# One low-rank product of three matmuls, moved by two steps in TensorE's program

## The chip, the core and the metric

The kernel runs on one core of a Trainium2 chip. The metric is device time in microseconds (us), taken over repeated runs; the profiled execution gives the trace. Ratios are computed as the mean time of one kernel's fast runs over that of the other's fast runs of the same rounds, so they are not quite the ratio of the medians quoted beside them.

## The reference

For each of 8 batches (3136 rows, 256 columns): squared-ReLU attention gated by `u`, then a mixer with a rank-32 product over the rows and a two-layer ReLU network over the columns.

```python
scores = (1 / S) * z @ z.T                  # z: 3136 x 64
x = u * (np.maximum(scores, 0) ** 2 @ v)    # attention, gated
h = x.T @ U @ V                             # rank 32 over the rows
y = x + h.T
out = y + np.maximum(y @ w_ch1, 0) @ w_ch2  # 256 -> 1024 -> 256
```

## The kernel before

The attention of batch b and the mixer of batch b - 1 are interleaved by hand: the order in which the program emits instructions is the order on each engine. The 3136 rows are 25 tiles, so a batch has 25 outputs of 25 steps each; a step is two matmuls, one on each half of TensorE's rows. Outputs come in pairs, and a pair accumulates in one of two sets of two banks of PSUM, the memory that takes TensorE's results (`ps` in the traces). The set that is not in use is "spare": the low-rank products of the mixer borrow it. (`...` stands for lines left out, and the pieces stand apart in the kernel.)

```python
def spare():
    return sets[(opened[0] + (0 if acc else 1)) % 2]

def open_pair(b, o):                        # at step 0 of a pair: takes the spare set
    acc[pair_of(o)[0]] = sets[opened[0] % 2]
    opened[0] += 1

def low_rank(b, c, ps=None, turned=True):   # the rank-32 product of one chunk of tiles
    ts = chunks[c]                          # four tiles; three in chunk 3; two in chunk 6
    ps = spare() if ps is None else ps
    where = [(0, 0), (1, 0)] if len(ts) == 2 else [(0, 0), (0, 1), (1, 0), (1, 1)]
    order = sorted(zip(where, ts), key=lambda e: (e[0][1], e[0][0]))
    for (h, k), t in order:                 # h: bank and row half, k: half of the bank
        mm(out=ps[h][:, k * D : (k + 1) * D],
           lhsT=V_bf[halves[h], col(t) : col(t) + P], rhs=t1[b][halves[h], :],
           start=True, stop=True)
    ...
    for h in range(2):                      # VectorE reads bank 0, then bank 1
        ...
        nc.vector.tensor_tensor(out=q, in0=split(ps[h][:, : len(ks) * D]), in1=q, op=ALU.add)
    if turned:
        turn_x(b, c)                        # DMA transpose for the next layer

def _spread(main, filler):                  # score pieces, spread over an output's steps
    n, m = len(main), len(filler)
    k = 0
    for i, step in enumerate(main):
        step()
        while k < m and (2 * k + 1) * n <= (i + 1) * 2 * m:
            filler[k]()
            k += 1
    ...

# in the loop over batches b and outputs i:
ahead = dict(zip((2, 3, 6, 7, 10, 11, 14), range(NC)))    # output -> chunk
main = attend_steps(b, o)
if b and i in ahead:
    main.insert(17 if (i + (i > FIRST)) % 2 == 0 else 10, lambda c=ahead[i]: low_rank(b - 1, c))
_spread(main, fill)
```

So the third chunk's product stands late in output 6 and the fourth's at entry 10 of output 7, and both use the same spare set. A score piece is two matmuls (L298), a ReLU on ScalarE (L311) and a square on VectorE (L313).

## Time and profile before

| | before |
|---|---|
| median of the first three runs | 1002.39 us (1002.05 to 1003.09) |
| profiled span | 998.3 us |
| TensorE busy | 983.4 us, 99% |
| VectorE, ScalarE busy | 551.1 us, 612.2 us |

Read it as: TensorE sets the time, and only its own waits can be won. In the traces the line of an instruction tells what it is: L371 an output step, L298 a score piece, L531 a low-rank product, L545 its additions on VectorE, L405 the steps of output 12 (the tail tile), L563 and L610 the two layers of the mixer's network. `A` holds the squared scores, a `strip` is a part of `A` transposed by a DMA, `ut` is the mixer's input transposed by a DMA, and `o_sb` is the buffer from which the output is stored.

One measure is the time **from the start of the first chunk's product (output 2) to the start of the fifth's (output 10)** of the same batch. It holds the place of the change, and repeats to 0.01 us where nothing stray hits it. In the kernel before, the seven batches have 49.50, 49.50, 49.50, 49.51, 50.21, 49.50 and 49.50 us.

### The profile page before, as it was taken

Reading aid. Unit: us, or ns where it says so; the run is one execution under the profiler, and the core shown is the slowest. Engines: PE = TensorE matmul, PEld = TensorE weight load, DVE = VectorE, ACT = ScalarE, POOL = GpSimd, SP = SyncE. Lnnn points to the kernel's source line nnn. Section 1 sums busy time; section 2 is a strip of 40 time slices with the busy share of each in tenths; the row PEclk is TensorE's granted clock in tenths of the full one; section 3 lists DMA queues with packets and bytes.
Section 4 is the critical chain, followed back from the end, with each engine's and each line's share of the span. In section 5 each row is a group of like instructions: output and inputs, shape, how many; then the busy total and the mean of one; then the engine's idle time right before and its main releaser. Section 6 shows DMA issues by size and latency. Waiting matters only on the chain.

```text
span 998.3 us, 31020 instructions
## 1 busy us (share of the span) xinstructions
PE 983.4 (99%) x13688; PEld 776.5 (78%) x13688; DVE 551.1 (55%) x1003; ACT 612.2 (61%) x835; POOL 171.7 (17%) x317
## 2 busy tenths in 40 slices
PE   8899999999999999999999999999999999999998
PEld 6678777787778877788787887878877788787866
DVE  6878754467444665456644566445664457542352
ACT  8877764667645776466754667556674666643154
POOL 5111112111121211221112211112111120011000
PEclk9999999999999999999999999999999999999999
DMA  9999989899798999999999997989979998678533
GB/s 195 185 195 204 174 156 186 185 176 173 153 198 171 169 157 186 179 178 169 160 180 176 181 168 149 188 174 177 175 151 194 166 188 159 120 150 161 129 95 101
DMA packets 414790, 167.94 MB, mean 168 GB/s; under 512 B 389488, under 2 KB 399408, under 8 KB 414656
## 3 DMA queue, kind: packets, MB, share of 16 engines
q1 hardware_dynamic: 385424, 99.68, 62.3%
q0 software_dynamic: 29232, 66.28, 28.3%
q8 instruction: 107, 1.75, 0.7%
q14 instruction: 27, 0.22, 0.1%
HBM read 61.88 MB, written 25.69 MB: 88 GB/s over the span
## 4 chain that ended last, share of the span: by engine, by line
PE 91%; DVE 4%; ACT 3%; DMA 1%; issue 1%; POOL 0%; DVEq 0%; POOLq 0%
PE ps L371 47%; PE ps L563 17%; PE ps L610 17%; PE ps L298 6%; ACT A L311 2%; DVE A L313 2%; PE ps L405 1%; PE ps L531 1%; DVE x_bf L545 1%; DMA out_dram<-o_sb 1%; DMA strip<-A 1%; DVE both L386 1%; PE ps L479 1%; DVE x_bf L395 1%; PE ps L207 0%
## 5 line engine op out<-in xcount | busy, mean ns | idle before, releaser
L311 ACT ACTIVATE A<-ps 128x832 bf16<-128x832 f32 (+9 forms) x477 | 358.9, 769 | 155.4 <-PE ps L298 148.1
L371 PE MATMUL ps<-v,A 64*128 64x256 bf16 x4988 | 341.6, 269 | 1.8 <-DVE A L313 1.1
L313 DVE TENSOR_TENSOR A<-A 128x832 bf16<-128x832 bf16 (+9 forms) x477 | 244.7, 527 | 133.1 <-ACT A L311 130.0
L371 PE MATMUL ps<-v,strip 64*128 64x256 bf16 x4420 | 307.3, 269 | 3.4 <-DMA strip<-A 2.5
L371 PEld LDWEIGHTS <-A 64*128 64x128 bf16 x4988 | 246.3, 94 | 45.4 <-issue 10.0
L581 ACT ACTIVATE relu_bf<-ps 128x1024 bf16<-128x1024 f32 (+2 forms) x206 | 186.2, 911 | 140.0 <-PE ps L563 139.8
L371 PEld LDWEIGHTS <-strip 64*128 64x128 bf16 x4420 | 222.6, 94 | 37.2 <-DMA strip<-A 3.9
L624 DVE TENSOR_TENSOR o_sb<-ps,x_bf 128x512 f32<-128x512 f32 (+2 forms) x105 | 69.9, 665 | 243.7 <-PE ps L610 221.7
L610 PE MATMUL ps<-w_bf,relu_bf 128*128 128x256 bf16 (+1 forms) x1600 | 201.2, 273 | 0.0
L563 PE MATMUL ps<-ut,w_bf 128*128 128x512 bf16 (+2 forms) x896 | 198.6, 353 | 0.0
L610 PEld LDWEIGHTS <-relu_bf 128*128 128x128 bf16 (+1 forms) x1600 | 153.0, 98 | 45.6 <-issue 3.6
L563 PEld LDWEIGHTS <-w_bf 128*128 128x128 bf16 x896 | 84.9, 98 | 62.0 <-issue 6.9
L355 POOL DMA_DIRECT2D u_sb<-in_u_dram x96 | 53.7, 559 | 456.1 <-DVE x_bf L395 441.9
L298 PE MATMUL ps<-zT 64*128 64x416 bf16 (+8 forms) x812 | 131.6, 312 | 0.0
L385 ACT COPY both<-ps 128x512 f32<-128x512 f32 (+1 forms) x104 | 58.9, 566 | 72.9 <-PE ps L371 66.6
L637 POOL DMA_DIRECT2D out_dram<-o_sb x84 | 46.0, 548 | 276.2 <-DVE o_sb L624 272.9
L386 DVE TENSOR_TENSOR both<-ps,both 128x512 f32<-128x512 f32 (+1 forms) x104 | 69.3, 667 | 28.2 <-ACT both L385 27.5
L395 DVE TENSOR_TENSOR x_bf<-both,u_sb 128x512 bf16<-128x512 f32 (+1 forms) x104 | 69.8, 672 | 3.7
L545 DVE TENSOR_TENSOR x_bf<-ps,x_bf 128x512 bf16<-128x512 f32 (+1 forms) x112 | 65.5, 626 | 7.2 <-PE ps L531 7.1
L298 PEld LDWEIGHTS <-zT 64*128 64x128 bf16 x812 | 43.1, 94 | 4.0
L244 POOL DMA_DIRECT2D v<-in_v_dram x61 | 34.1, 561 | 0.8 <-DMA w_bf<-in_moe_w_ch_dram 0.7
L298 PE MATMUL ps<-relu_bf 64*128 64x416 bf16 (+9 forms) x121 | 22.2, 333 | 3.9 <-ACT A L311 3.3
(54 smaller groups left out, 208.0 us busy)
## 6 DMA issues: line engine op xcount, KB each, us to landing
u_sb<-in_u_dram POOLq DMA_DIRECT2D x96, 256.0 KB, 4.1
out_dram<-o_sb POOLq DMA_DIRECT2D x84, 256.0 KB, 3.3
v<-in_v_dram POOLq DMA_DIRECT2D x57, 192.0 KB, 4.8
strip<-A SPq DMA_TRANSPOSE x196, 5.5
out_dram<-o_sb SPq DMA_DIRECT2D x11, 256.0 KB, 2.0
z_c<-in_z_dram POOLq DMA_DIRECT2D x7, 384.0 KB, 5.9
u_sb<-in_u_dram POOLq DMA_DIRECT2D x16, 64.0 KB, 2.5
ut<-x_bf SPq DMA_TRANSPOSE x56, 3.7
```

Source lines behind the costliest of these rows:

```text
L298: mm(out=ps[:, k, :n], lhsT=zT[halves[k], j, :], rhs=zT_flat[halves[k], c : c + n], start=True, stop=True,)
L311: nc.scalar.activation(out=dst, in_=src, func=AF.Relu, scale=sc)
L313: nc.vector.tensor_tensor(out=dst, in0=dst, in1=dst, op=ALU.mult)
L371: mm(out=acc[t0][h][:, (o - t0) * D : (o - t0 + 1) * D], lhsT=w[halves[h]], rhs=v_both[b % 2][halves[h], j, :], start=start, stop=stop, **kw,)
L385: nc.scalar.copy(out=both[:, :w], in_=banks[1][:, :w])
L386: nc.vector.tensor_tensor(out=both[:, :w], in0=banks[0][:, :w], in1=both[:, :w], op=ALU.add)
L395: nc.vector.tensor_tensor(out=x_at(b, t0, n), in0=split(both[:, :w]), in1=u_sb[:, :n, :].rearrange("p t (a c) -> p t a c", c=P), op=ALU.mult,)
L545: nc.vector.tensor_tensor(out=q, in0=split(ps[h][:, : len(ks) * D]), in1=q, op=ALU.add)
L563: mm(out=ps[i][:, :w] if apart else ps[:, i, :w], lhsT=w1_bf[:, db, (hp + i) * P : (hp + i + 1) * P], rhs=uT[c][:, db, len(chunks[c]) * P ...
L581: nc.scalar.activation(out=relus[c][:, hp : hp + 2, :w], in_=ps[:, :, :w], func=AF.Relu)
L610: mm(out=ps[r, k * D : (k + 1) * D], lhsT=relus[c][:, ht, q : q + (TAIL if two else P)], rhs=w2_bf[:, ht, :], start=(ht < 1 + two), stop=( ...
L624: nc.vector.tensor_tensor(out=o_sb[:p].rearrange("p t (a c) -> p t a c", c=P), in0=split(ps[:p, k0 * D : (k + 1) * D]), in1=x_at(b, t, nk) ...
```

## The change

The intent: the fourth chunk's product stands at TensorE waiting for its banks; put it two steps later and let those steps run in front of it.

```diff
             main = attend_steps(b, o)
             if b and i in ahead:
-                main.insert(17 if (i + (i > FIRST)) % 2 == 0 else 10, lambda c=ahead[i]: low_rank(b - 1, c))
+                at = 17 if (i + (i > FIRST)) % 2 == 0 else 12 if i == 7 else 10
+                main.insert(at, lambda c=ahead[i]: low_rank(b - 1, c))
             _spread(main, fill)
```

## The prediction

> **What bounds the kernel now.** I read the page first, then the list of waits of the whole run, then the waits of TensorE alone in stretches, then the timeline around the instruction that the diff moves, for all seven batches that have it. The page:
>
> ```profile
> span 998.3 us, 31020 instructions
> PE 983.4 (99%) x13688; PEld 776.5 (78%) x13688; DVE 551.1 (55%) x1003; ACT 612.2 (61%) x835; POOL 171.7 (17%) x317
> PEclk9999999999999999999999999999999999999999
> PE 91%; DVE 4%; ACT 3%; DMA 1%; issue 1%; POOL 0%; DVEq 0%; POOLq 0%
> ```
>
> TensorE is busy for 99% of the span at the full granted clock, and 91% of the chain that ended last is TensorE. Every other engine has 39% or more free. So time is gained only where TensorE does less work or stands still for less time. That it stands still so rarely makes its few waits readable one by one. The complete list for TensorE's matmuls is:
>
> ```profile
> PE ps L298 <- ACT A L311: 3.3, 5, 1.0
> PE ps L371 <- DMA strip<-A: 2.5, 1, 2.5
> PE ps L371 <- DVE A L313: 2.0, 4, 0.9
> PE ps L207 <- DVE zT L204: 1.3, 1, 1.3
> PE ps L531 <- DVE x_bf L545: 1.1, 7, 0.2
> PE ps L371 <- DVE o_sb L624: 0.5, 1, 0.5
> PE ps L298 <- ACT relu_bf L231: 0.4, 1, 0.4
> ```
>
> (Columns: total us, times, longest.) Asked in stretches of the span, the start-up before 80 us holds all of these but two: one wait of 0.5 us near 645 us, and the row of L531. L531 is the low-rank product, and seven waits fit batches 1 to 7, each of which holds the product that the diff moves. The timeline of TensorE and of VectorE in batch 2 shows it (start, duration, engine, line):
>
> ```profile
> 258.43 0.71 PE L371 MATMUL ps<-v,A 64*128 64x256 bf16 x10
> 258.98 0.27 PE L531 MATMUL ps<-t_sb,V_bf 64*128 64x256 bf16 x1
> 259.40 0.29 PE L531 MATMUL ps<-t_sb,V_bf 64*128 64x256 bf16 x2 [0.16 <-DVE x_bf L545]
> 259.51 0.40 PE L371 MATMUL ps<-v,A 64*128 64x256 bf16 x4
> 259.73 0.33 PE L298 MATMUL ps<-zT 64*128 64x352 bf16 x2
> ```
>
> ```profile
> 258.67 0.68 DVE L545 TENSOR_TENSOR x_bf<-ps,x_bf 128x512 bf16<-128x512 f32 x1
> ```
>
> The fourth chunk's product has three matmuls. The first, into bank 0 of the spare pair, starts at 258.98. The second, into bank 1, starts only at 259.40, 0.05 us after VectorE ends (258.67 + 0.68 = 259.35) the second addition of the THIRD chunk's product, which used the same two banks half an output earlier. It is a wait for a buffer. The same pair of starts, 0.42 to 0.43 us apart, stands in all seven batches (137.77 and 138.19 in the first, 865.97 and 866.39 in the last), so one figure holds for all.
>
> How much does a site lose? Not the 0.16 us in brackets: that counts only from the modelled end of the first matmul (258.98 + 0.27). A full product of four matmuls in the same batch starts at 256.62, and the next output matmul at 256.83: 0.21 us for four, in two side-by-side pairs. Here three matmuls need the same two turns, so the next output matmul should start near 258.98 + 0.21 = 259.20 and starts at 259.51. **Loss: 0.31 us a site, 7 x 0.31 = 2.2 us in all.** No change to this wait can give more.
>
> **What the Trainium skill says.** "PSUM — Partial Sum Buffer", section "PSUM bank collisions raise a hardware error", asks for semaphores by bank: a matmul may not write a bank while VectorE reads it. The trace agrees: the first matmul (bank 0, freed 0.6 us earlier) goes, the second waits, and only until the addition that reads its bank is over. "TensorE: Matmul & The Clock Gate", section "The mechanism", says that matmuls are strict FIFO. So independent output matmuls that stand behind the blocked one in the program can't overtake it; the trace agrees, as the L371 matmuls at 259.51 need nothing from it and still come after. This is why order in the program matters here at all. "Perfetto Trace Analysis", section "Tensor Engine Instruction (MATMUL, LD_WEIGHTS)", says that a matmul's end is estimated and not observed; hence I count from start to start, and the bracket's 0.16 against 0.31 is this case's measure of the difference.
>
> **The change part by part.** It removes and adds no instruction. `at` becomes 12 instead of 10 for output 7 alone, in batches 1 to 7 (ahead holds chunk 3 there).
>
> (1) Order on TensorE. Output 7 has 25 steps of two matmuls each, one per row half, and with the product 26 entries. Three score pieces are spread over it (1408 columns in two, 256 in one): by the rule in _spread they follow entries 4, 12 and 21. Before: steps 0 to 9, product, steps 10 and 11, second score piece, step 12. After: steps 0 to 11, product, second score piece, step 12. So exactly two steps, four matmuls, pass in front of the product.
>
> (2) Order elsewhere. The additions of the product still come after the square of score piece 1 and before that of piece 2 on VectorE; ScalarE, the DMA queues and the transposes keep their order wholly. VectorE's addition that frees the bank hangs on nothing moved, so it still ends near 259.35 on the old clock.
>
> (3) What two steps fill. The trace has x16 output matmuls as 0.87 us from issue to issue (for example in the chain of waits), so a step is 0.87 / 8 = 0.109 us and two are 0.22 us. They would run at 258.98 and 259.09. The first product matmul goes at 259.20, the second still waits until 259.40, the third follows at 259.42, and the score piece starts at about 259.51 where it started at 259.73. **Gain 0.22 us of the 0.31; 0.09 us stays as a wait, because 12 is not quite late enough.**
>
> (4) Does the gain survive what comes next? VectorE doesn't get earlier at once: it squares until about 259.9 and then adds for the product (259.87 to 260.89), set by its own queue. Its next squares were ready to start at 260.89 in any case. At the close of outputs 6 and 7 it has caught up:
>
> ```profile
> 262.09 0.69 DVE L386 TENSOR_TENSOR both<-ps,both 128x512 f32<-128x512 f32 x1 [0.24 <-ACT both L385]
> ```
>
> It idles 0.24 us there for ScalarE, which waits for TensorE; with TensorE 0.22 us earlier this idle shrinks to about nothing and nothing is late. The spare banks are opened for outputs 8 and 9 after 261.9, about 1 us after the product's last addition. Between two such sites TensorE has no listed wait but the single 0.5 us, so nothing is there to take the gain back.
>
> (5) Sum: 7 x 0.22 = 1.5 us. 1002.39 - 1.53 = **1000.9 us**, a gain of 0.15%.
>
> **The rivals.** *A: the wait moves on and nothing is gained.* VectorE is the laggard at this site: the chain of waits runs through two squares and both additions for 2.1 us before it comes back to TensorE, so TensorE catches up on VectorE's schedule, and a gain here could reappear as a wait at the next meeting (close of the pair, bank reuse for output 8). For: that chain. Against: the 0.24 us of VectorE idle at the close, the 1 us of room before the banks are reopened, and that TensorE shows no other wait in a batch. It would leave 1002.4 us. *B: the whole wait goes.* If the time lost beyond the two steps is partly hidden (third matmul overlapped with what follows on the other row half), the gain would be up to 0.31 us a site: 1002.39 - 2.2 = 1000.2 us. For: the remaining 0.09 us is less than one step. Against: the bank is not free before 259.35, and the first product matmul would come at 259.20. *C: the later product delays the third-chunk-to-fourth transposes and so the mixer's first product of chunk 3.* For: the transpose into ut for chunk 3 is issued at 264.78 and takes about 4.1 us to land, near 268.9. Against: its additions are set by VectorE's queue and don't get later; the transpose is then held in its queue by two others (a strip at 260.71, z at 262.93), so even 0.2 us would vanish; and the matmuls that read it start at 271.40, 2.5 us after. It would take a slip of over 2 us; then each 0.1 us more would cost 0.7 us in all. I give it almost nothing. *D: a different order of the same work changes a modelled pattern of row halves.* The product's third matmul uses one row half; what follows is now a score pair instead of an output step, both of which use both halves, so at most a fraction of a step, 0.1 us a site or 0.7 us in all, either way.
>
> **Range and chances.** The whole wait is 2.2 us, 0.2% of the time; no mechanism that I can name reaches 2% (20 us) in either direction. The three runs before spread over 1.0 us (1002.05 to 1003.09), which is two thirds of the predicted gain. The low end is B with a little spread, 1000.0; the high end is A with a little less than no gain, 1002.2. Faster by over 2%: 0.01. Within 2%: 0.98. Slower: 0.01. The question that is really open is whether 1.5 us shows above the spread.
>
> **What the profile after would show.** Step 1: in each of the seven sites the output steps before the product number two more (four matmuls), and a score pair follows the product directly. Step 3: the distance from the first to the second product matmul shrinks from 0.42 to about 0.20 us, less than a matmul's modelled length of 0.27, so the row "PE ps L531 <- DVE x_bf L545" should vanish from the waits although a wait of 0.2 us is still there. Step 4: no new TensorE wait in a batch, and the distance from one batch's site to the next, 121.2 us in the trace before (380.42 to 501.63), shrinks to about 121.0. The seven together: the span falls by about 1.5 us from 998.3. It would be wrong if the distance of batches stays at 121.2 although the gap in the site has shrunk (A), if the score piece after the product waits for something (a new row of L298), or if the up product of chunk 3 shows a wait for ut (C).

## The result, and the profile after

Six runs each: the changed kernel 1001.36 us (998.93 to 1003.71), the kernel before 1002.74 us (1001.74 to 1004.45); ratio 0.9985, 95% interval 0.9966 to 1.0003: the same at 2%. The predicted ratio was 1000.9 / 1002.39 = 0.9985 too, but single runs lie several us apart, so the total alone would prove nothing. The trace does.

The timeline of TensorE at the place of the change, changed kernel, batch 2 (start, duration, engine and line, with the count behind x):

```profile
262.80 0.49 PE L371 MATMUL ps<-v,A 64*128 64x256 bf16 x6
263.12 0.49 PE L531 MATMUL ps<-t_sb,V_bf 64*128 64x256 bf16 x3
263.44 0.33 PE L298 MATMUL ps<-zT 64*128 64x352 bf16 x2
263.59 0.29 PE L371 MATMUL ps<-v,A 64*128 64x256 bf16 x2
```

The product is one group now, with no bracket, and the score pair follows it directly. What was 0.53 us from the first product matmul to the next other matmul (258.98 to 259.51) is 0.32 us here (263.12 to 263.44). Three matmuls need 0.21, so 0.11 us a batch is still lost, without any mark in the trace.

The complete list of TensorE's matmul waits in the changed kernel (us in total, times, longest):

```profile
PE ps L298 <- ACT A L311: 6.1, 6, 2.8
PE ps L371 <- DMA strip<-A: 3.4, 2, 2.4
PE ps L207 <- DVE zT L204: 1.3, 1, 1.3
PE ps L371 <- DVE A L313: 1.1, 3, 0.5
PE ps L223 <- DVE z_bf L188: 0.6, 1, 0.6
PE ps L298 <- ACT relu_bf L231: 0.4, 1, 0.4
PE ps L371 <- DMA v<-in_v_dram: 0.3, 1, 0.3
```

The row of L531 is gone. Everything that is listed lies in the start-up, before 100 us.

First to fifth product: 49.28 us in six of the seven batches (49.57 in the first, where an up product, L563, starts 0.3 us later after the second chunk's product than in the other batches; the trace puts that down to the transpose `ut`, but it is in no list). The clean figures differ by 0.22 us, as predicted; seven times that is 1.5 us.

Yet the span of this very trace is longer: 1000.2 against 998.3 us. Cut it at two products to see where:

| trace | start to first product | from there to the fifth product of batch 7 | rest | span |
|---|---|---|---|---|
| before | 111.29 | 777.70 | 109.31 | 998.3 |
| changed | 115.15 | 775.78 | 109.32 | 1000.2 |

The middle, where the change is, is 1.92 us shorter: 1.5 us of it is the change, and the rest are stray waits that only one of the traces has. The start-up was 3.86 us longer, though the change touches nothing before output 7 of batch 1. Most of it is TensorE's own waiting there: without L531 and o_sb, the listed waits of the kernel before (in the prediction) sum to 9.5 us, those of the changed kernel to 13.2. The chain that ended last, in shares of the span, points at the same stretch. Before:

```profile
PE ps L371 47%; PE ps L563 17%; PE ps L610 17%; PE ps L298 6%; ACT A L311 2%; DVE A L313 2%; PE ps L405 1%; PE ps L531 1%; DVE x_bf L545 1%; DMA out_dram<-o_sb 1%; DMA strip<-A 1%; DVE both L386 1%; PE ps L479 1%; DVE x_bf L395 1%; PE ps L207 0%
```

After:

```profile
PE ps L371 48%; PE ps L610 17%; PE ps L563 17%; PE ps L298 6%; DMA strip<-A 3%; ACT A L311 2%; PE ps L531 1%; PE ps L405 1%; DMA z_c<-in_z_dram 1%; PE ps L479 1%; DVE A L313 1%; DMA ut<-x_bf 0%; DVE both L386 0%; PE ps L462 0%; POOL v L244 0%
```

In the changed kernel's execution the chain runs through DMA for longer (strips 3%, z 1%) than in the other (strips 1%); why, is not shown. The additions L545, 1% of the chain before, are no longer among its lines, which fits the change.

### The profile page after: what moved, and what is told of

Same layout as the page of the kernel before. It is cut to its first block, busy times and chain, and to the rows that moved or that the text cites. A ratio compares the mean times of both kernels' runs of the same rounds, so it can differ in the third digit from the quotient of the medians.

```text
span 1000.2 us, 31020 instructions
## 1 busy us (share of the span) xinstructions
PE 982.9 (98%) x13688; PEld 778.4 (78%) x13688; DVE 551.0 (55%) x1003; ACT 612.5 (61%) x835; POOL 171.6 (17%) x317
## 4 chain that ended last, share of the span: by engine, by line
PE 92%; DMA 4%; ACT 2%; DVE 1%; POOL 0%; issue 0%; DVEq 0%; ACTq 0%; POOLq 0%
PE ps L371 48%; PE ps L610 17%; PE ps L563 17%; PE ps L298 6%; DMA strip<-A 3%; ACT A L311 2%; PE ps L531 1%; PE ps L405 1%; DMA z_c<-in_z_dram 1%; PE ps L479 1%; DVE A L313 1%; DMA ut<-x_bf 0%; DVE both L386 0%; PE ps L462 0%; POOL v L244 0%
## 5 line engine op out<-in xcount | busy, mean ns | idle before, releaser
L371 PE MATMUL ps<-v,A 64*128 64x256 bf16 x4988 | 340.9, 269 | 1.5 <-DVE A L313 1.1
L371 PE MATMUL ps<-v,strip 64*128 64x256 bf16 x4420 | 307.6, 269 | 3.4 <-DMA strip<-A 3.4
L371 PEld LDWEIGHTS <-A 64*128 64x128 bf16 x4988 | 247.7, 94 | 44.0 <-issue 10.2
L371 PEld LDWEIGHTS <-strip 64*128 64x128 bf16 x4420 | 223.8, 94 | 36.4 <-DMA strip<-A 4.5
L624 DVE TENSOR_TENSOR o_sb<-ps,x_bf 128x512 f32<-128x512 f32 (+2 forms) x105 | 69.9, 666 | 241.9 <-PE ps L610 216.9
L563 PE MATMUL ps<-ut,w_bf 128*128 128x512 bf16 (+2 forms) x896 | 198.7, 353 | 0.1
L563 PEld LDWEIGHTS <-w_bf 128*128 128x128 bf16 x896 | 84.8, 98 | 62.4 <-issue 6.7
L545 DVE TENSOR_TENSOR x_bf<-ps,x_bf 128x512 bf16<-128x512 f32 (+1 forms) x112 | 65.5, 626 | 6.9 <-PE ps L531 6.8
```

Source lines behind the costliest of these rows:

```text
L371: mm(out=acc[t0][h][:, (o - t0) * D : (o - t0 + 1) * D], lhsT=w[halves[h]], rhs=v_both[b % 2][halves[h], j, :], start=start, stop=stop, **kw,)
L563: mm(out=ps[i][:, :w] if apart else ps[:, i, :w], lhsT=w1_bf[:, db, (hp + i) * P : (hp + i + 1) * P], rhs=uT[c][:, db, len(chunks[c]) * P ...
L624: nc.vector.tensor_tensor(out=o_sb[:p].rearrange("p t (a c) -> p t a c", c=P), in0=split(ps[:p, k0 * D : (k + 1) * D]), in1=x_at(b, t, nk) ...
```

## The experiments

All outputs are right. In each table row, "first to fifth" is the value of the batches without a stray wait, and "batches" says how many of the seven these are.

| kernel | first to fifth, us | batches | time ratio (95% interval) |
|---|---|---|---|
| before | 49.50 | 6 | 1 |
| changed | 49.28 | 6 | 0.9985 (0.9966 to 1.0003) |
| changed, again | 49.28 | 6 | 0.9994 (0.9974 to 1.0015) |
| changed, a third time | 49.28 | 6 | 0.9969 (0.9932 to 1.0007) |
| `at5` | 50.05 | 7 | 1.0059 (1.0029 to 1.0089) |
| `at13` | 50.19 | 7 | 1.0029 (1.0012 to 1.0046) |
| `thirteen` | 49.17 | 6 | 0.9960 (0.9945 to 0.9976) |
| `thirteen`, again | 49.18 | 5 | 0.9954 (0.9915 to 0.9993) |
| `third_later` | 49.28 | 4 | one look: 1002.79 us |
| `third_later`, again | 49.28 | 4 | one look: 1008.43 us |
| `score_banks` | 49.57 | 6 | one look: 999.96 us |
| `both_sites` | 49.18 | 7 | 0.9990 (0.9974 to 1.0005) |

By the threshold of 2% every one of these ratios is "the same"; what follows rests on the batches.

### at5: the suspected wait made longer

```diff
-                at = 17 if (i + (i > FIRST)) % 2 == 0 else 12 if i == 7 else 10
+                at = 17 if (i + (i > FIRST)) % 2 == 0 else 5 if i == 7 else 10
```

> The fourth chunk's product at entry 5 of output 7, five steps earlier than in the kernel before, instead of two later; the order on VectorE and ScalarE is unchanged. My theory (TensorE stands at the second matmul until VectorE's last addition of the third chunk's product, a time that doesn't depend on where the product stands): every step that no longer stands in front of it adds 0.109 us to the wait, so 0.55 us a batch more than before. From the start of the first chunk's product to that of the fifth's: 49.50 us before, 49.28 in the changed kernel, 50.05 here. Seven waits on L545 of about 0.7 us each after the modelled end (1.1 us in total before, about 5 here). Time: 3.8 us over before (about 1.0038). Rival (VectorE sets the pace here and TensorE only meets it later, so the place of the wait doesn't matter): 49.50 and the time of before.

50.04 or 50.05 us in all seven batches, 0.55 more than before, which is what five steps of 0.109 us give. The timeline of TensorE, batch 2:

```profile
260.40 0.27 PE L531 MATMUL ps<-t_sb,V_bf 64*128 64x256 bf16 x1 [0.21 <-DVE x_bf L545]
261.00 0.28 PE L531 MATMUL ps<-t_sb,V_bf 64*128 64x256 bf16 x2 [0.33 <-DVE x_bf L545]
261.10 0.40 PE L371 MATMUL ps<-v,A 64*128 64x256 bf16 x4
```

Now the first matmul waits as well, for the addition that reads bank 0, and the second for the one that reads bank 1. The list has 14 waits of 3.8 us in all, where I had expected seven of about 5. The decisive number is the second matmul's start counted from the third chunk's product (258.21 here, 256.62 before): 2.79 us here, 2.78 before. In the changed kernel it is 2.79 as well (260.54 to 263.33). The release is at a fixed time; only what stands in front of it changes. The time (1.0059) has the expected 1.0038 inside its interval.

### third_later: what fixes the release

```diff
-                at = 17 if (i + (i > FIRST)) % 2 == 0 else 12 if i == 7 else 10
+                at = (19 if i == 6 else 17) if (i + (i > FIRST)) % 2 == 0 else 12 if i == 7 else 10
```

> The changed kernel with the THIRD chunk's product also two steps later (entry 19 of output 6 in place of 17), so that the two products are again as far apart on TensorE as in the kernel before. My theory (VectorE's queue of squares sets when the additions of the third product end, and TensorE's distance is nothing): VectorE gets to those additions only about 1 us after the matmuls, so the matmuls have room; first to fifth product stays 49.28 us, the second matmul of the fourth product still starts 0.2 us after the first, no wait listed on L545. Rival (it is the distance of the two products that counts): 49.50, and the 0.42 us and the seven listed waits return.

The distance from the third to the fourth product on TensorE is now 2.36 us (258.23 to 260.59), as it was before the change (256.62 to 258.98). Still the gain stands: 49.28 us, and the product is one group without a listed wait.

```profile
258.23 0.38 PE L531 MATMUL ps<-t_sb,V_bf 64*128 64x256 bf16 x4
258.53 1.02 DVE L313 TENSOR_TENSOR A<-A 128x768 bf16<-128x768 bf16 x2
259.47 1.28 DVE L545 TENSOR_TENSOR x_bf<-ps,x_bf 128x512 bf16<-128x512 f32 x2
260.59 0.49 PE L531 MATMUL ps<-t_sb,V_bf 64*128 64x256 bf16 x3
```

VectorE (DVE) is the reason: when the third product's matmuls are through, it has squares to do first, and gets to the additions at 259.47, 1.24 us after the product began. The queue of VectorE sets the release, not the distance of the two products.

Three batches of this trace were longer (50.07, 50.03, 51.31).

> The kernel with the third product two steps later a second time: in its first trace four of seven batches had 49.28 us and three had 50.0 to 51.3. My theory: the three came from the stores of the output (two waits for DVE o_sb of 2.5 us in all), which strike any of the kernels in some batches; most batches have 49.28 again, and others than before are long. If the third product's new place causes them, the same three or more are long again.

Four batches had 49.29 or 49.28 in each trace, but the long ones were batches 2, 3 and 5 in the first and 3, 5 and 6 in the second: in part the same, against what I expected. The listed waits are a store-bound addition (L371 on DVE o_sb L624: 2.5 us in the first trace, 0.4 in the second), a wait of L563 for the transpose `ut` of 0.6 us in batch 3 of both, and 3.8 us of L405 in the second, which fall outside the measured stretch. In batch 3 the excess lies before the third product, so not at what was moved in that batch. Whether the place of the third product invites such waits stays open.

### thirteen: all of the wait

The product after 13 steps, yet in front of the second score piece, so that VectorE and ScalarE keep their order.

```diff
-                main.insert(at, lambda c=ahead[i]: low_rank(b - 1, c))
+                if i == 7:
+                    s = main[12]
+                    main[12] = lambda s=s, c=ahead[i]: (s(), low_rank(b - 1, c))
+                else:
+                    main.insert(at, lambda c=ahead[i]: low_rank(b - 1, c))
```

> The product after 13 steps of output 7, but in front of the second score piece, so that VectorE and ScalarE keep their order. My theory: the product's first matmul comes at about the time that the bank of the second falls free, so all of the 0.31 us is won: first to fifth product 49.19 us (49.50 before, 49.28 in the changed kernel), 2.2 us under before in all, no wait on L545. Rival (the 0.09 us left in the changed kernel is the third matmul's own slot on one row half and no wait): 49.28.

```profile
257.96 0.71 PE L371 MATMUL ps<-v,A 64*128 64x256 bf16 x10
258.50 0.38 PE L531 MATMUL ps<-t_sb,V_bf 64*128 64x256 bf16 x3
258.71 0.33 PE L298 MATMUL ps<-zT 64*128 64x352 bf16 x2
```

From the product to the next matmul 0.21 us: nothing is lost, and the 0.11 us left in the changed kernel was wait. The second matmul still has to wait for its bank (VectorE's addition ends at 258.55, the matmul starts at 258.60, again 2.79 us after the third product), but by now that fits beside the third matmul, which takes its turn on the other row half. First to fifth 49.17 us in six batches (49.28 in the other), 0.33 less than before. 7 x 0.33 = 2.3 us would give a ratio of 0.9977; measured was 0.9960, with that value just outside its interval (0.9945 to 0.9976).

> The kernel with 13 steps in front of the product a second time. Its first timing (0.9960) was better than the 0.33 us a batch seen in its trace give (7 x 0.33 = 2.3 us, 0.9977). My theory: the trace is right and the first timing was lucky by 1 to 2 us: 49.17 us again, and 0.9977 within the interval. If the kernel gains somewhere that I haven't seen, 0.996 comes again.

Again 49.18 us in five batches (50.10 and 49.57 in two with stray waits), and 0.9954 (0.9915 to 0.9993). The better ratio came twice, against my expectation. The sum of the trace is inside the second interval; if there is a gain beyond it, I have not found where. `both_sites` below has batches of the same length and came out at 0.9990, so the whole times don't settle it. This version is clear of 1 in both series, so faster than the kernel before, though by far less than 2%; that it beats the changed kernel by 0.1 us a batch is shown by the traces.

### at13: later still, and worse

```diff
-                at = 17 if (i + (i > FIRST)) % 2 == 0 else 12 if i == 7 else 10
+                at = 17 if (i + (i > FIRST)) % 2 == 0 else 13 if i == 7 else 10
```

> The product at entry 13, one step later than in the changed kernel; but there the second score piece of output 7 stands after entry 12 and so comes in front of the product, and its square in front of the product's additions on VectorE. My theory: the wait at the product is gone (0.31 us), but the additions wait for that square (which waits for ScalarE) and end about 1.1 us later, so the first matmuls of output 8, which reopen the same banks, wait about 0.4 us for L545: first to fifth product about 49.6 us, seven new waits of L371 on L545, the time no better than before (0 to +1 us). Rival (later is simply better): no wait, 49.19 us, 2.2 us under before.

On TensorE this product stands after the same 13 steps as in `thirteen`. But the second score piece now comes before it, and with it that piece's square on VectorE. Result: 50.19 us, 0.69 worse than before and 1.01 worse than `thirteen`. TensorE and VectorE, batch 2:

```profile
261.08 0.38 PE L531 MATMUL ps<-t_sb,V_bf 64*128 64x256 bf16 x3
261.19 1.14 PE L371 MATMUL ps<-v,strip 64*128 64x256 bf16 x16
...
262.08 0.53 DVE L313 TENSOR_TENSOR A<-A 128x704 bf16<-128x704 bf16 x1 [0.50 <-ACT A L311]
...
262.52 1.01 DVE L545 TENSOR_TENSOR x_bf<-ps,x_bf 128x512 bf16<-128x512 f32 x2
...
263.26 1.03 PE L371 MATMUL ps<-v,A 64*128 64x256 bf16 x10 [0.54 <-DVE x_bf L545]
```

The product itself doesn't wait. VectorE stands 0.50 us for ScalarE, squares, and begins the additions only at 262.52; the first step of output 8, which takes the same banks for its accumulation, has to wait until the first of them ends (262.52 + 0.68 = 263.20) and starts at 263.26. I had the mechanism right and its size 0.6 us too small, because I had put the start of output 8 too late (see below). The time, 1.0029, has an interval (to 1.0046) that just misses the 1.0048 of 7 x 0.69 us.

### score_banks: other banks instead of another place

The fourth product back at entry 10 (that line is cut here), but in a pair of the banks in which score pieces alternate.

```diff
+        if len(ts) == 3 and b + 1 < B:
+            pair = pair_psum()
+            ps = [pair[:, 0, :], pair[:, 1, :]]
         ps = spare() if ps is None else ps
```

> The fourth product in its old place (entry 10), but into a pair of the banks in which the score pieces alternate, so that it shares no bank with the third product. My theory: the wait at the product is gone (its matmuls start together), but the third score piece of output 7 then needs that pair again and waits until the product's additions end, about 0.4 us; the loss only changes its place: a new row L298 on DVE L545, first to fifth product 49.4 to 49.7 us. Rival (it is the bank alone, and another bank cures it): 49.19 us and no new wait.

```profile
259.12 0.38 PE L534 MATMUL ps<-t_sb,V_bf 64*128 64x256 bf16 x3
...
261.08 0.23 PE L298 MATMUL ps<-zT 64*128 64x128 bf16 x2 [0.19 <-DVE x_bf L548]
```

(The edit shifts line numbers: L534 is the product, L548 its additions.) The product runs through in one go, and the third score piece waits for the same additions instead, in all seven batches. 49.57 us, slightly worse than before. The wait was moved, not removed: what makes a bank late is VectorE's queue, and the bank that the product borrows here is needed again before VectorE has given it back.

### both_sites: the same cure at output 3

As `thirteen` (its lines are cut here), and the second chunk's product at entry 12 of output 3 too.

```diff
-                at = 17 if (i + (i > FIRST)) % 2 == 0 else 12 if i == 7 else 10
+                at = 17 if (i + (i > FIRST)) % 2 == 0 else 12 if i == 3 else 10
```

> As thirteen, and the second chunk's product two steps later too (entry 12 of output 3), whose third matmul starts 0.15 us after the first in the kernel before where 0.21 us hold all four in other places (0.28 us to the next output matmul). My theory: about 0.07 us more a batch, first to fifth product 49.12 us, 2.7 us under before in all. Rival: the second site has no wait that counts, 49.19 as in thirteen.

No further gain: 49.17 or 49.18 us, as the rival said, but for a reason that I had not named. At output 3 itself the matmuls no longer wait: from the product to the next matmul 0.27 us becomes 0.22. What was won is gone at the start of output 4 (TensorE and VectorE of `both_sites`):

```profile
235.26 0.38 PE L531 MATMUL ps<-t_sb,V_bf 64*128 64x256 bf16 x4
...
236.11 1.28 DVE L545 TENSOR_TENSOR x_bf<-ps,x_bf 128x512 bf16<-128x512 f32 x2
...
237.18 0.27 PE L371 MATMUL ps<-v,A 64*128 64x256 bf16 x1
...
237.45 0.40 PE L371 MATMUL ps<-v,A 64*128 64x256 bf16 x4
```

Output 4 reopens the banks. Its first matmul starts at 237.18, the second, into bank 1, only at 237.45, after the second addition has ended (236.11 + 1.28 = 237.39). Counted from the first chunk's product (235.26 is the second's; the first's is at 232.55) that is 4.90 us. In the kernel before and in `thirteen` it is 4.89 and 4.90 us (232.50 to 237.39, 231.69 to 236.59), but there the first matmul of output 4 came later, so the gap between the two was 0.20 us and is now 0.27. TensorE arrives earlier and waits longer: VectorE's additions bind a second time right after, and a gain on TensorE in front of them is worth nothing. The gap of 0.20 us lies outside the lists of waits, as it is shorter than a matmul's modelled length.

### The changed kernel twice more

> The changed kernel once more, beside the others. My theory: first to fifth product 49.28 us in each of the batches 1 to 7 as in its first trace; the time 1.5 us under before (0.9985), with single runs some us apart. I expect that the spread of the runs comes from the start-up before the first product (111.3 us in the one trace, 115.2 in the other) and not from the batches. If the spread is in the batches, their lengths differ from trace to trace instead.

> The changed kernel a third time, for the sum. My theory: 49.28 us from the first to the fifth product in most batches, whatever the time of the whole is; the time 0.9985 of before with an interval of some 0.002 to either side, because single runs differ by up to 4 us for other reasons.

49.28 us again in most batches of both traces (49.50 in one and 49.57 in another). The middle part is 775.80 and 775.79 us, against 775.78 in the first trace. The start-up is 112.21 and 117.05 us. So the spread of these three lies in the start-up for the most part: over the twelve traces it takes 110.8 to 117.1 us, which no change touches. Stray waits add to it: the middle of `thirteen` has 774.79 us in one trace and 777.27 in the other. The longer ones are listed as an output step behind an addition into o_sb (L624), L405 behind L545, or L563 behind `ut`; those of 0.2 to 0.3 us in the changed kernel's traces are in no list. In the kernel before, VectorE waits six times, 14.1 us in all, for a store of an earlier output to release the buffer o_sb; that this delays the rest is likely, but no run tests it.

## Why the prediction was right

**The bound.** Right: TensorE sets the time; the change took 0.22 us a batch from TensorE, and a batch became shorter by that. From one batch's site to the next it is 120.99 us in the undisturbed batches, where 121.0 was predicted (121.21 before).

**Step 1 and 2, the order.** Right: two steps more in front of the product, the score pair directly behind; VectorE, ScalarE and the queues keep their order.

**Step 3, what two steps fill.** Right: 0.22 us predicted, 49.50 - 49.28 = 0.22 measured; a rest of 0.09 us predicted, 0.11 measured. The frozen release was the point that everything hung on, and it is the best proven: 2.78 us after the third product before, 2.79 in `at5`, in the changed kernel and in `thirteen`, with the fourth product at four different places.

**The loss at the site.** 0.31 us were read from starts, and `thirteen` recovered 0.33. The bracket of the trace said 0.16.

**Step 4, does the gain survive.** The answer was right, in part by luck, for the argument had three errors. First, the spare banks are not reopened "after 261.9" but at 261.24 in the kernel before, where output 8 begins; an output reads its blocks from `A` first and then from strips, and the `A` lines from 261.24 on are already output 8's. So the room between the last addition and the reopening was not 1 us but 0.35 (260.89 to 261.24). The changed kernel leaves 0.13 (264.82 to 264.95) and `thirteen` 0.05 (260.08 to 260.13): the gain that could survive was only just as large as the wait to be removed. The same error made `at13` 0.6 us worse than expected. Second, VectorE's idle time before the close of outputs 6 and 7 did not shrink to nothing:

```profile
265.80 0.69 DVE L386 TENSOR_TENSOR both<-ps,both 128x512 f32<-128x512 f32 x1 [0.24 <-ACT both L385]
```

It is 0.24 us as before. VectorE had caught up one instruction earlier: its last square before the close waited for ScalarE in both kernels, so it moved forward with TensorE. Third, "no listed wait" was taken for no wait. In the kernel before, two more matmuls of every batch start 0.05 us after the addition L545 that frees their bank and are in no list: one of the second chunk's product (234.99 to 235.14 from the matmul before it) and one where output 4 opens (237.19 to 237.39). The second is the one that took the gain back in `both_sites`.

**The rivals.** A, that nothing is gained because VectorE sets the pace, failed here but came true at output 3 (`both_sites`) and, in another form, in `at13`. B, that the whole wait goes, failed: it took a thirteenth step. C failed: no matmul of the changed kernel's batches has a listed wait for `ut`; the unlisted 0.3 us of batch 1 lies in front of the moved product. D, a change through the row halves, is at most the 0.02 us between the predicted and the measured rest.

**Time.** 1000.9 us predicted, 1001.36 measured. That the two are so near is luck: the other two series of the changed kernel have medians of 1002.59 and 1000.68 us. The three series of the changed kernel (0.9985, 0.9994, 0.9969) all have 0.9985 inside their intervals, and all have 1 inside them too. The total is consistent with the prediction and doesn't prove it; the lengths of the batches do.

## What to carry to other kernels

When an in-order engine that sets the time waits at an instruction, put independent work of that engine in front of it, about as much as the wait is long, and leave the releasing engine's order alone: the same step on TensorE won 0.33 us or lost 0.69 depending on whether a square slipped in front of the product's own additions. Before counting the gain, find the next place where the two engines meet and measure the room there, since it caps what survives. And where the whole time varies more than the gain, measure between two marks of the same batch in the trace.

## What the Trainium skill lacked or had wrong

- "Perfetto Trace Analysis", section "Tensor Engine Instruction (MATMUL, LD_WEIGHTS)": it says that a matmul's end is estimated, but not what this does to waits. A bubble is hidden by up to a matmul's modelled length (0.27 us here): 0.32 us lost was listed as 0.16, and the 0.11 us left in the changed kernel as nothing.
- "PSUM — Partial Sum Buffer", section "PSUM bank collisions raise a hardware error": no figure for how soon a matmul follows a reader of its bank. Here it started 0.05 to 0.06 us after the end of VectorE's addition in the kernel before (259.35 to 259.40), in `thirteen` (258.55 to 258.60), in `both_sites` (237.39 to 237.45) and in `at13` (263.20 to 263.26).
